# Gate copy on ScalarE, running maximum's VectorE work one step later, and six small tables in PSUM, in an attention and mixture-of-experts kernel

## The chip, the cores and the metric

One core of a Trainium2 chip runs the whole kernel. The metric is the device time of one execution in microseconds (us), and of several executions the median. The core has TensorE (PE in the profile), VectorE (DVE), ScalarE (ACT), GpSimd (POOL) and SyncE (SP), which here only issues transfers. SBUF is the large on-chip memory that all of them use; PSUM is the small one of eight banks into which TensorE writes its products, and from which VectorE and ScalarE read them.

## What is computed

```python
B, H, S, D = (8, 8, 576, 64)                      # q, k, v
scores = q @ k.T / sqrt(D)
kth    = np.partition(scores, -32)[..., -32]      # keep the 32 largest scores of a row
attn   = softmax(where(scores >= kth, scores, -1e9))
x      = (attn @ v).transpose(0, 2, 1, 3).reshape(4608, 512)
logits = x @ w_gate                               # 8 experts
e      = argmax(logits, axis=1);  p = softmax(logits)[e]
out    = p * (relu(x @ w1[e]) @ w2[e])            # F = 1024, one expert per token
```

All of it is in float32.

## The kernel before

**Attention.** The 64 heads of 8 batches give 288 units of 128 rows by 576 scores. The main loop has 144 steps (0 to 143, with a few more to drain), and each step handles two units, so that a batch is 18 steps. In step t the code issues, in this order: the exponentials of step t-4 (ScalarE, `exps`, tile `et` from the PSUM tile `tt`), the marks of step t-2 (`softmax`: ScalarE's Sign into `sg`, then GpSimd's `sb<-sb,sg` in L456), the scores of step t+3 (`scores`: TensorE into `ps`, copied by ScalarE to `sb` in L369, and the rest in L388), the product with V of step t-5 (`av`, into `px`), and the nine transposes of step t-3 (`transp`, TensorE into `tt`). Then VectorE finds the 32 largest values of each row of step t: 21 MAX8 over pieces of a row (L1026), then MAX8 and MATCH_REPLACE over the candidates (L1034).

**Small jobs.** Everything else is written as generators ("jobs") that a planner starts at due times and advances once a step. They do not issue at once: `vec(f, ...)`, `act(f, ...)`, `pe(f, ...)` and `pool(f, ...)` append to the queues `dq`, `aq`, `pq` and `gq`, and the loop empties them at fixed places. `dq` is emptied between VectorE's instructions of L1034, one job instruction behind each from the third on. All job instructions have the line of the helper, L265. The jobs that matter here:

- `j_find`, once for each batch: `r_key` from the table `idx1`; then counts on TensorE, ScalarE's `stat`, and `settle`; a step or more later `r_sl` and `r_qx` from the table `slots`.
- `settle`: `mm` (a reduce of a TensorE product in PSUM, the running maximum over the partitions), the release of the bank, and `shift` from the table `level`. A first `settle` stands in step 1 of the loop.
- `j_route`, once for each batch, behind its attention: `oh` from the table `edesc`, `hist` from the table `valid`, and `po` from the table `ebase`. It sorts the tokens to the experts.
- `j_rows`: `xm`, `lp`, `xl` and `lpl`, scaled copies out of PSUM of attention's result turned by TensorE against `turner`. The last columns of `turner` hold the gate's weights `wg`; two VectorE copies in L993, ahead of the loop, put them there.

**PSUM before.** `three` (tile `tt`, 9 blocks of 128 columns, that is 1152 float32 of a partition, 512 to a bank), `ps` (two banks), `px` (one), and two banks `pt` that jobs take and release.

**What sets the order.** Each engine runs its instructions in the order in which the code issued them, and waits on semaphores. There are no priorities. Behind the loop the flag `att_open[0]` is set to False, the last jobs run among the instructions of the experts' part, and that part runs from about 756 us to the end. It is TensorE's products of L1154 (`ph`) and L1169 (`y`), with each weight and each activation split into two parts.

Of the kernel before, what the change touches and what calls it, by code (L numbers as in the profile page):

```python
# [8 lines left out]
F32 = mybir.dt.float32  # L9
# [4 lines left out]
AF = mybir.ActivationFunctionType  # L14
OP = mybir.AluOpType
# [7 lines left out]
TOPK = 32  # L23
# [25 lines left out]
def attention_moe(ctx, tc, q, k, v, w_gate, w1, w2, out):  # L49
    nc = tc.nc  # L50
    B, H, S, D = q.shape
    HP = H // 2
    DM = H * D
    E = w_gate.shape[1]
# [11 lines left out]
    ahead, part_of = {}, []  # L66
# [5 lines left out]
    KB = MAIN + 1  # L72
# [23 lines left out]
    psum = att.enter_context(tc.tile_pool(name="psum", bufs=1, space=PSUM))  # L96
# [22 lines left out]
    turner = consts.tile([128, HP, RW], F32, name="turner")  # L119
# [8 lines left out]
    wg = consts.tile([128, DC, E], F32, name="wg")  # L128
# [128 lines left out]
    VQ, CNT, NB = {}, {}, {}  # L257
# [6 lines left out]
    def later(queue):  # L264
        return lambda f, *a, **k: queue.append(lambda: f(*a, **k))  # L265
# [13 lines left out]
    def flush(queue):  # L279
        while queue:  # L280
            queue.pop(0)()
# [16 lines left out]
        return free.pop(0)  # L298

    NB9 = 2 * MAIN + 1  # L300
    three = psum.tile([128, NB9 * 128], F32, name="tt")

    MAINS = psum.tile([128, 2, 512], F32, name="ps")

# [132 lines left out]
    def spread(pt):  # L437
        pe(nc.tensor.matmul, pt[:, 0:128], top.to_broadcast([128, 128]), ident, start=True, stop=True)

    def settle(pt, ns, done):  # L440
        mm = jobs.tile([128, 1], F32, name="mm")
        vec(nc.vector.tensor_reduce, mm, pt[:, 0:128], axis=AX.X, op=OP.max)
        vec(done)
        k = len(ns)
        vec(nc.vector.scalar_tensor_tensor, shift[:, ns[0]:ns[0] + k], slope[:, None, :].to_broadcast([128, k, 3]), mm,
            level[:, None, :].to_broadcast([128, k, 3]), op0=OP.mult, op1=OP.add)

    SHIFTED = {0, 1, 2, 3}

# [165 lines left out]
    def j_find(b):  # L615
# [2 lines left out]
        while (b + 1) * NLT // (2 * NT) - 1 not in CHECKED:  # L618
            yield
        key = sm("r_key", [128, NLT])  # L620
        vec(nc.vector.scalar_tensor_tensor, key, CNT[b], float(2 * TOPK - S), idx1, op0=OP.not_equal, op1=OP.mult)
        vec(nc.vector.max, rhs[:, :, 0], key)
        ok = sm("r_ok", [128, 9], BF)
        vec(nc.vector.tensor_scalar, ok[:, 0:8], rhs[:, :, 0], 0.0, None, op0=OP.is_gt, op1=OP.add,
# [8 lines left out]
        act(nc.scalar.activation, stat[:, b], pr[:, 0:3], AF.Copy)  # L633
        if 2 * b + 4 < NQ:
            spread(pr[:, 128:256])
            settle(pr[:, 128:256], [2 * b + 4, 2 * b + 5], leave)
            SHIFTED.update([2 * b + 4, 2 * b + 5])
        else:
            act(leave)
        yield need(slack=1)  # L640
        yield need(dve=1.3)
        sl = sm("r_sl", [128, 8], BF)
        vec(nc.vector.scalar_tensor_tensor, sl, slots[:, 0:8], stat[:, b, 0:1], ok[:, 0:8], op0=OP.add, op1=OP.mult)
        oh = sm("r_qx", [128, 512]).bitcast(BF).rearrange("p (j x) -> p j x", j=8)
        vec(nc.vector.tensor_tensor, oh, slots[:, None, :].to_broadcast([128, 8, 128]),
            sl[:, :, None].to_broadcast([128, 8, 128]), op=OP.is_equal)
        yield need(spot=1, pe=0.5)
        pl, leave = spot("li")
# [141 lines left out]
    def j_route(b):  # L790
# [19 lines left out]
        vec(nc.vector.tensor_reduce, lg, ll.rearrange("p i (h e) -> p i e h", h=H), axis=AX.X, op=OP.add)  # L810
        vec(nc.vector.tensor_reduce, mx, lg, axis=AX.X, op=OP.max)
        vec(nc.vector.tensor_tensor, sh, lg, mx[:, :, None].to_broadcast([128, KB, E]), op=OP.subtract)
        vec(nc.vector.scalar_tensor_tensor, oh, sh, 0.0, edesc, op0=OP.is_equal, op1=OP.mult)
        vec(nc.vector.tensor_reduce, fm, oh, axis=AX.X, op=OP.max)
        vec(nc.vector.tensor_tensor, oh, oh, fm[:, :, None].to_broadcast([128, KB, E]), op=OP.is_equal)
        yield need(dve=0.6)
        vec(nc.vector.tensor_tensor, hist[:, :, KB + 1:].rearrange("p e c -> p c e"), oh, valid, op=OP.mult)
        win = bass.AP(hist.tensor, hist.offset, [list(hist.ap[0]), list(hist.ap[1]), [1, KB + 1], [1, KB + 1]])
        vec(nc.vector.tensor_reduce, cum, win, axis=AX.X, op=OP.add)
        vec(nc.vector.tensor_copy, hist[:, :, KB], cum[:, :, KB])  # L820
# [12 lines left out]
        pool(nc.gpsimd.iota, pay[:, :, 3:4], pattern=[[0, KB], [0, 1]], base=0, channel_multiplier=0)  # L833
        pos = small("pos", [128, KB], I32)
        posf = small("posf", [128, KB])
        vec(nc.vector.tensor_tensor, po, po, ebase, op=OP.add)
        vec(nc.vector.tensor_tensor, po, po, oh, op=OP.mult)
        vec(nc.vector.tensor_reduce, posf, po, axis=AX.X, op=OP.add)
        vec(nc.vector.tensor_scalar, pos, posf, float(E * N - 1), None, op0=OP.min)
# [88 lines left out]
    def prep(p):  # L928
        if p < P:
            start(f"prep{p % 2}", j_prep(p))  # L930
# [47 lines left out]
        parts_w(k, [SPARE.pop(0) for _ in range(4)], nc.vector)  # L978

    SPARE = []  # L980
    prep(0)
    drain()
    prep(1)
# [5 lines left out]
            for queue in (gq, pq, aq, dq):  # L989
                flush(queue)  # L990
    drain()
    for h in range(2):
        nc.vector.tensor_copy(turner[h * D:(h + 1) * D, :, 128 + h * E:128 + (h + 1) * E], wg[h * D:(h + 1) * D])  # L993
    nc.sync.dma_start(xs[0:PAD, :], zero[:, 0:DM])
    nc.sync.dma_start(atab.rearrange("(p t) a -> p t a", p=128), attr)
    for i in range(B):
# [8 lines left out]
    for t in range(steps + LAG + TD + 4):  # L1005
        n, s = divmod(t, NT)
        if delayed:
            delayed[0](*delayed[1])
        if grp(t - LAG - TD - 1):
            exps(t - LAG - TD - 1)  # L1010
        if grp(t - LAG):
            softmax(t - LAG, grp(t - LAG), 0)
        scores(grp(t + LA))
        if grp(t - LAG):
            softmax(t - LAG, grp(t - LAG), 1)
        if grp(t - LAG - TD - 2):
            av(t - LAG - TD - 2, grp(t - LAG - TD - 2))
        scores_left(grp(t + LA))
        if grp(t - LAG - TD):
            transp(t - LAG - TD)  # L1020
        flush(pq)
        flush(aq)
        one, two, last = topk(t, grp(t)) if grp(t) else ([], [], None)
        for m in range(max(len(one), 1)):
            if m < len(one):
                one[m][0](*one[m][1])  # L1026
        delayed = last
        if t == 1:
            settle(first_pt, [0, 1, 2, 3], lambda: release(first_pt))
            mine_, dq[:] = dq[:], []  # L1030
            flush(mine_)
        mine, dq[:] = dq[:], []
        for m, (f, a) in enumerate(two):
            f(*a)  # L1034
            if mine and m >= 2:
                mine.pop(0)()
        flush(mine)
        if t == 0:
# [456 lines left out]
```

## Time and profile before

| what | value |
|---|---|
| median of 3 runs | 1278.19 us (1275.56 to 1279.88) |
| the profiled execution | 1278.04 us, of it 1276.2 us from the first to the last instruction |
| TensorE's granted clock in it, mean | 0.988 |
| busy: PE, DVE, ACT, POOL | 1209.7, 1020.9, 832.6, 840.1 us |
| VectorE's first MAX8 on scores | at 12.76 us |
| first instruction of the experts' part on TensorE (`mt`) | at 755.62 us |

In the profile a row of the timeline is: start in us, length in us, engine, line, operation, output<-inputs, sizes, count, and in brackets the idle time just ahead of it with what ended it. A group's row has the minimum, median and maximum length in ns instead. A timeline row with a count can span several instructions.

### The profile page before, as it was taken

How to read it: one execution, taken by the hardware profiler on the slowest of the kernel's cores; microseconds unless marked ns; L12 is line 12 of the kernel's file. 1: busy time of each engine (PE TensorE's matmuls, PEld its weight loads, DVE VectorE, ACT ScalarE, POOL GpSimd, SP SyncE). 2: the span in 40 equal slices, each digit the busy share in tenths (PEclk: the TensorE clock that was granted, in tenths of full speed). 3: DMA queues.
4: the chain of work that ended last, by engine and by line, in shares of the span. 5: the costliest groups of instructions: out<-in, count | busy, mean ns of one | idle time of the engine just before them, and what ended most of it. 6: DMA issues, size and time to landing. Idle time of an engine off the chain costs nothing.

```text
span 1276.2 us, 31656 instructions
## 1 busy us (share of the span) xinstructions
PE 1209.7 (95%) x9126; PEld 963.3 (75%) x9126; DVE 1020.9 (80%) x6898; ACT 832.6 (65%) x1699; POOL 840.1 (66%) x1213
## 2 busy tenths in 40 slices
PE   6999999999999999999999879899999999999997
PEld 3667667766676767666667668789899998899996
DVE  7999999999999999999999986755674333446555
ACT  4999798998898898898998853333333232333433
POOL 4676666767977967967968858766554242455654
PEclk8999999999999999999999999899999999999999
DMA  6765564654655655665654635745665243556773
GB/s 172 233 179 184 165 204 145 191 180 154 190 177 165 196 169 167 194 176 164 187 172 144 184 101 147 223 125 173 167 192 162 75 135 93 155 164 193 228 213 112
DMA packets 276758, 215.37 MB, mean 169 GB/s; under 512 B 136617, under 2 KB 218713, under 8 KB 276576
## 3 DMA queue, kind: packets, MB, share of 16 engines
q1 hardware_dynamic: 265840, 190.11, 50.5%
q0 software_dynamic: 9504, 22.86, 5.7%
q8 instruction: 74, 1.21, 0.4%
q14 instruction: 108, 0.88, 0.2%
q10 hardware_dynamic: 1232, 0.30, 0.1%
HBM read 106.69 MB, written 107.90 MB: 168 GB/s over the span
## 4 chain that ended last, share of the span: by engine, by line
DVE 43%; PE 42%; ACT 5%; POOL 4%; issue 3%; DMA 2%; SPq 1%; POOLq 0%; ACTq 0%; DVEq 0%
DVE cand L1026 21%; PE ph L1154 17%; PE y L1169 17%; DVE cand L1034 9%; DVE vq L1034 8%; PE pt L265 2%; ACT sg L455 2%; POOL sb L456 2%; PE mt L1134 1%; PE px L478 1%; PE ps L367 1%; DVE xm L265 1%; POOL wl L958 1%; PE tt L462 1%; ACT sb L369 1%
## 5 line engine op out<-in xcount | busy, mean ns | idle before, releaser
L456 POOL TENSOR_TENSOR sb<-sb,sg 128x576 f32<-128x576 f32 x288 | 370.1, 1302 | 48.3 <-ACT sg L455 41.1
L1026 DVE MAX8 cand<-sb 128x8 f32<-128x52 f32 (+2 forms) x3024 | 366.3, 207 | 0.0
L958 POOL TENSOR_TENSOR wl<-r,wh 128x512 fp32r<-128x512 f32 x118 | 153.2, 1299 | 207.2 <-DVE wh L957 201.8
L455 ACT ACTIVATE sg<-sb,nb 128x576 int8<-128x576 f32 x288 | 229.0, 795 | 49.5 <-POOL sb L456 48.9
L1155 ACT ACTIVATE hh<-ph 128x256 fp32r<-128x256 f32 (+3 forms) x136 | 58.4, 429 | 247.6 <-PE ph L1154 247.5
L478 PEld LDWEIGHTS px<-et,rv 128*64 128x64 f32 x2688 | 129.9, 137 | 119.0 <-ACT xt L265 47.6
L1034 DVE MAX8 vq<-cand 128x8 f32<-128x22 f32 (+7 forms) x1152 | 200.5, 205 | 0.0
L367 PE MATMUL ps<-qk 64*128 64x512 f32 (+1 forms) x576 | 185.0, 650 | 3.9 <-ACT sb L369 3.2
L462 PE MATMUL tt<-turner,sb 128*128 128x128 f32 x1296 | 173.5, 276 | 14.8 <-POOL sb L456 10.4
L1156 DVE SCALAR_TENSOR_TENSOR hl<-ph,hh 128x256 fp32r<-128x256 f32 (+3 forms) x136 | 65.0, 478 | 150.8 <-ACT hh L1155 150.5
L468 ACT ACTIVATE et<-tt,shift 128x1152 f32<-128x1152 f32 x144 | 178.4, 1239 | 2.9 <-PE tt L462 2.9
L478 PE MATMUL px<-et,rv 128*64 128x128 f32 (+1 forms) x2688 | 163.1, 267 | 11.4 <-ACT xt L265 8.7
L1154 PE MATMUL ph<-xh,wh 128*128 128x256 f32 (+3 forms) x536 | 169.8, 317 | 0.0
L1154 PE MATMUL ph<-xh,wl 128*128 128x256 f32 (+3 forms) x536 | 165.8, 309 | 0.0
L1154 PE MATMUL ph<-xl,wh 128*128 128x256 f32 (+3 forms) x536 | 165.3, 308 | 0.0
L462 PEld LDWEIGHTS tt<-turner,sb 128*128 128x128 f32 x1296 | 145.8, 142 | 24.9 <-POOL sb L456 18.5
L1034 DVE MATCH_REPLACE8 cand<-vq,cand 128x22 f32<-128x22 f32 (+2 forms) x864 | 158.4, 189 | 0.0
L369 ACT ACTIVATE sb<-ps 128x1024 f32<-128x1024 f32 x144 | 149.1, 1036 | 8.7 <-PE ps L367 8.5
L1169 PE MATMUL y<-wh,hl 128*128 128x512 f32 x324 | 128.3, 396 | 1.4 <-DVE hl L1156 1.4
L1169 PE MATMUL y<-wl,hh 128*128 128x512 f32 x324 | 128.2, 396 | 0.0
L1169 PE MATMUL y<-wh,hh 128*128 128x512 f32 x324 | 128.2, 396 | 0.0
L1154 PEld LDWEIGHTS ph<-xh,wh 128*128 128x128 f32 x536 | 101.7, 190 | 4.2 <-issue 1.3
(260 smaller groups left out, 2178.4 us busy)
## 6 DMA issues: line engine op xcount, KB each, us to landing
r<-in_moe_w_dram SPq DMA_DIRECT2D x236, 256.0 KB
sc<-sb SPq DMA_DIRECT2D x128, 288.0 KB
sc<-sb SPq DMA_DIRECT2D x128, 256.0 KB
rv<-in_v_dram SPq DMA_DIRECT2D x32, 256.0 KB
xs<-xm SPq DMA_DIRECT2D x16, 512.0 KB
rq<-in_q_dram SPq DMA_DIRECT2D x60, 128.0 KB
rk<-in_k_dram SPq DMA_DIRECT2D x60, 128.0 KB
sc<-sb SPq DMA_DIRECT2D x32, 144.0 KB
```

What stands on the lines that cost most here:

```text
L367: nc.tensor.matmul(MAINS[:, n], qk[:, 0, w], qk[:, 1, 2 * LEFT:], start=True, stop=True)
L369: nc.scalar.activation(bass.AP(EX[-1].tensor, EX[-1].offset, [list(EX[-1].ap[0]), [S + LEFT, 2], [1, M]]), MAINS, AF.Copy)
L455: nc.scalar.activation(upper(SG[i]), SB[u], AF.Sign, bias=nb[:, i, 1:2], accum_out=CNT[b][:, 2 * lt + i:2 * lt + i + 1])
L456: nc.gpsimd.tensor_tensor(SB[u], SB[u], SG[i], op=OP.add)
L462: nc.tensor.matmul(tt[:, c], x[:, c * 128:(c + 1) * 128], ident, start=True, stop=True, is_transpose=True)
L468: nc.scalar.activation(ET[t], three.rearrange("p (c q) -> p c q", c=NB9), AF.Exp, bias=shift[:, t // NT, 0:1], scale=0.125)
L478: yield lambda kb=kb, blk=blk: nc.tensor.matmul(px[h * 64:(h + 1) * 64], block(rv, p % 2, kb if kb < MAIN else MAIN + n, h), et[:, blk, q] ...
L958: ((other or nc.gpsimd) if i else nc.vector).tensor_tensor(lo, r, hi, op=OP.subtract)
L1026: one[m][0](*one[m][1])
L1034: f(*a)
L1154: nc.tensor.matmul(ph, a[:, c, :], x[:, c, s], start=(m == 0), stop=(m == len(seq) - 1))
L1169: nc.tensor.matmul(PY[u, t], a[:, s], x, start=(f == 0 and m == 0), stop=(f == FC - 1 and m == 2))
```

## The change

1. **Gate copy.** The two VectorE copies `turner<-wg` ahead of the loop are gone. Behind step 3 two ScalarE copies do the same.
2. **Running maximum.** In `j_find`, the instructions that `settle` gives to VectorE go to a second queue, `late_dq`, which is added to `dq` a step later. The first `settle` stands in step 2 instead of step 1.
3. **Tables.** The PSUM tile `tt` grows from 1152 to 1536 columns, three whole banks. Its last 384 columns take float32 copies of six tables (`idx1`, `slots`, `level`, `edesc`, `valid`, `ebase`; 287 columns). `const(name)` gives the PSUM copy while `att_open[0]` holds, and the SBUF table after that. ScalarE makes the copies: `level` ahead of the loop, the others with the queue that is filled in step 4. So the third bank holds the ninth transposed block of `tt` and the tables.

```diff
-    three = psum.tile([128, NB9 * 128], F32, name="tt")
+    spare = psum.tile([128, 3 * 512], F32, name="tt")
+    three = spare[:, 0:NB9 * 128]
+    TABLE = {}
+    o = NB9 * 128
+    for name, x in (("idx1", idx1), ("slots", slots), ("level", level), ("edesc", edesc), ("valid", valid), ("ebase", ebase)):
...
+        y = spare[:, o:o + n]
+        TABLE[name] = (x, y if len(x.shape) == 2 else y.rearrange("p (a b) -> p a b", b=x.shape[2]))
+        o += n
+    def const(name):
+        return TABLE[name][1 if att_open[0] else 0]
...
+    late_dq = []
-    def settle(pt, ns, done):
+    def settle(pt, ns, done, vec=vec):
...
-            level[:, None, :].to_broadcast([128, k, 3]), op0=OP.mult, op1=OP.add)
+            const('level')[:, None, :].to_broadcast([128, k, 3]), op0=OP.mult, op1=OP.add)
...
-            settle(pr[:, 128:256], [2 * b + 4, 2 * b + 5], leave)
+            settle(pr[:, 128:256], [2 * b + 4, 2 * b + 5], leave, later(late_dq))
...
-        vec(nc.vector.tensor_tensor, hist[:, :, KB + 1:].rearrange("p e c -> p c e"), oh, valid, op=OP.mult)
+        vec(nc.vector.tensor_tensor, hist[:, :, KB + 1:].rearrange("p e c -> p c e"), oh, const("valid"), op=OP.mult)
...
-        vec(nc.vector.tensor_tensor, po, po, ebase, op=OP.add)
+        vec(nc.vector.tensor_tensor, po, po, ebase if ahead and b > min(ahead) else const('ebase'), op=OP.add)
...
+    nc.scalar.activation(const("level"), level, AF.Copy)
     prep(0)
...
-    for h in range(2):
-        nc.vector.tensor_copy(turner[h * D:(h + 1) * D, :, 128 + h * E:128 + (h + 1) * E], wg[h * D:(h + 1) * D])
...
-        if t == 1:
+        if t == 2:
             settle(first_pt, [0, 1, 2, 3], lambda: release(first_pt))
             mine_, dq[:] = dq[:], []
             flush(mine_)
         mine, dq[:] = dq[:], []
+        dq += late_dq
+        late_dq.clear()
...
+        if t == 3:
+            for h in range(2):
+                r = slice(h * D, (h + 1) * D)
+                nc.scalar.activation(turner[r, :, 128 + h * E:128 + (h + 1) * E], wg[r], AF.Copy)
+        if t == 4:
+            for name in ("idx1", "slots", "edesc", "valid", "ebase"):
+                act(nc.scalar.activation, const(name), TABLE[name][0], AF.Copy)
```

`idx1` in `r_key`, `slots` in `r_sl` and `r_qx`, and `edesc` in `oh` become `const(...)` in the same way.

The order of TensorE's, GpSimd's and SyncE's instructions is the same as before. On ScalarE and VectorE three places show what moved. In these rows a name with a number is one of several buffers; `tt` as an input of a VectorE instruction is a table's copy, and what stands in brackets are the engines on whose semaphores an instruction waits.

ScalarE at the end of step 5 and the start of step 6, before:

```order
L455 ACTIVATE sg_145,cnt<-sb,nb_230 128x576 [waits Pool_49]
L388 ACTIVATE sb<-px 128x128 [waits PE_49]
L265 ACTIVATE qk_224<-pt_246 128x512 [waits PE_49]
L468 ACTIVATE et<-tt,shift 128x1152
L455 ACTIVATE sg_143,cnt<-sb,nb_230 128x576 [waits Pool_49]
```

The same place now:

```order
L471 ACTIVATE sg_145,cnt<-sb,nb_230 128x576 [waits Pool_49]
L402 ACTIVATE sb<-px 128x128 [waits PE_49]
L265 ACTIVATE tt<-idx_127 128x36 [waits PE_49,Activation_49]
L265 ACTIVATE tt<-slots 128x128 [waits Activation_49]
L265 ACTIVATE tt<-edesc 128x40 [waits Activation_49]
L265 ACTIVATE tt<-valid 128x40 [waits Activation_49]
L265 ACTIVATE tt<-ebase 128x40 [waits Activation_49]
L265 ACTIVATE qk_224<-pt_247 128x512 [waits PE_49]
L484 ACTIVATE et<-tt,shift 128x1152 [waits Activation_49]
L471 ACTIVATE sg_143,cnt<-sb,nb_230 128x576 [waits Pool_49]
```

Five table copies stand in one row there, each waiting for the one ahead of it.

VectorE in step 21, the first `mm` and `shift` of `j_find`, before:

```order
L1034 MATCH_REPLACE cand_2014<-vq,cand_2014 128x22 [waits DVE_49]
L265 TENSOR_REDUCE mm<-pt_246 128x1 [waits Activation_49]
L1034 MATCH_REPLACE cand_2015<-vq,cand_2015 128x20 [waits DVE_49]
L1034 MAX vq<-cand_2014 128x8 [waits DVE_49]
L265 SCALAR_TENSOR_TENSOR shift<-slope,mm,level 128x6 [waits DVE_49]
L1034 MAX vq<-cand_2015 128x8 [waits DVE_49]
```

Now, in step 22:

```order
L1051 MATCH_REPLACE cand_2099<-vq,cand_2099 128x22 [waits DVE_49]
L265 TENSOR_REDUCE mm<-pt_247 128x1 [waits Activation_49]
L1051 MATCH_REPLACE cand_2100<-vq,cand_2100 128x20 [waits DVE_49]
L1051 MAX vq<-cand_2099 128x8 [waits DVE_49]
L265 SCALAR_TENSOR_TENSOR shift<-slope,mm,tt 128x6 [waits DVE_49,PE_49,Activation_49]
L1051 MAX vq<-cand_2100 128x8 [waits DVE_49]
```

`mm` and `shift` stand one step later, and `shift` now waits for TensorE and ScalarE too, which write and read the same banks of `tt`. `r_key`, `r_sl`, `oh`, `hist` and one `po` have the same two new waits: for the last nine transposes and the last `et` that were issued ahead of them.

VectorE in step 20, `r_key` now (before, it waits for Activation_49 and Pool_49 alone):

```order
L1051 MAX vq<-cand_1932 128x8 [waits DVE_49]
L1051 MAX vq<-cand_1933 128x8 [waits DVE_49]
L1051 MATCH_REPLACE cand_1932<-vq,cand_1932 128x22 [waits DVE_49]
L265 SCALAR_TENSOR_TENSOR r_key<-cnt,tt 128x36 [waits PE_49,Activation_49,Pool_49]
L1051 MATCH_REPLACE cand_1933<-vq,cand_1933 128x20 [waits DVE_49]
```

The wait for PE there is for the transposes of step 17, issued in step 20.

ScalarE at the end of the attention, steps 144 and 145, before:

```order
L265 ACTIVATE xt<-px 128x256 [waits PE_49]
L468 ACTIVATE et<-tt,shift 128x1152 [waits PE_49]
L455 ACTIVATE sg_143,cnt<-sb,nb_232 128x576 [waits Pool_49]
L455 ACTIVATE sg_145,cnt<-sb,nb_232 128x576 [waits Pool_49]
L265 ACTIVATE xt<-px 128x64 [waits PE_49]
L265 ACTIVATE xt<-px 128x64
L955 ACTIVATE rv_13337<-rq 128x512 [waits DMAHW6_49]
L468 ACTIVATE et<-tt,shift 128x1152 [waits PE_49]
```

The same place now:

```order
L265 ACTIVATE xt<-px 128x256 [waits PE_49]
L484 ACTIVATE et<-tt,shift 128x1152 [waits DVE_49]
L471 ACTIVATE sg_143,cnt<-sb,nb_232 128x576 [waits Pool_49]
L471 ACTIVATE sg_145,cnt<-sb,nb_232 128x576 [waits Pool_49]
L265 ACTIVATE xt<-px 128x64 [waits PE_49]
L265 ACTIVATE xt<-px 128x64
L971 ACTIVATE rv_13343<-rq 128x512 [waits DMAHW6_49]
L484 ACTIVATE et<-tt,shift 128x1152 [waits DVE_49]
```

Nothing moved, but both `et` now wait for VectorE: the first for `oh`, which stands in VectorE's row of step 143, the second for `hist`, which follows that row. There are five or six such `et` in a batch, each behind a table's reader of the step before.

More of the change, by code (lines that the diff above doesn't have):

```diff
@@ L300, in attention_moe @@
     NB9 = 2 * MAIN + 1
-    three = psum.tile([128, NB9 * 128], F32, name="tt")
+    spare = psum.tile([128, 3 * 512], F32, name="tt")
[3 more added lines that the diff above has]
+    for name, x in (("idx1", idx1), ("slots", slots), ("level", level), ("edesc", edesc), ("valid", valid), ("ebase", ebase)):
+        n = 1
+        for d in x.shape[1:]:
+            n *= d
+        y = spare[:, o:o + n]
+        TABLE[name] = (x, y if len(x.shape) == 2 else y.rearrange("p (a b) -> p a b", b=x.shape[2]))
+        o += n
+    assert o <= 3 * 512
+    def const(name):
+        return TABLE[name][1 if att_open[0] else 0]
     MAINS = psum.tile([128, 2, 512], F32, name="ps")
@@ L620, in j_find @@
         key = sm("r_key", [128, NLT])
-        vec(nc.vector.scalar_tensor_tensor, key, CNT[b], float(2 * TOPK - S), idx1, op0=OP.not_equal, op1=OP.mult)
+        vec(nc.vector.scalar_tensor_tensor, key, CNT[b], float(2 * TOPK - S), const('idx1'), op0=OP.not_equal, op1=OP.mult)
         vec(nc.vector.max, rhs[:, :, 0], key)
@@ L642, in j_find @@
         sl = sm("r_sl", [128, 8], BF)
-        vec(nc.vector.scalar_tensor_tensor, sl, slots[:, 0:8], stat[:, b, 0:1], ok[:, 0:8], op0=OP.add, op1=OP.mult)
+        vec(nc.vector.scalar_tensor_tensor, sl, const('slots')[:, 0:8], stat[:, b, 0:1], ok[:, 0:8], op0=OP.add, op1=OP.mult)
         oh = sm("r_qx", [128, 512]).bitcast(BF).rearrange("p (j x) -> p j x", j=8)
-        vec(nc.vector.tensor_tensor, oh, slots[:, None, :].to_broadcast([128, 8, 128]),
+        vec(nc.vector.tensor_tensor, oh, const('slots')[:, None, :].to_broadcast([128, 8, 128]),
             sl[:, :, None].to_broadcast([128, 8, 128]), op=OP.is_equal)
@@ L812, in j_route @@
         vec(nc.vector.tensor_tensor, sh, lg, mx[:, :, None].to_broadcast([128, KB, E]), op=OP.subtract)
-        vec(nc.vector.scalar_tensor_tensor, oh, sh, 0.0, edesc, op0=OP.is_equal, op1=OP.mult)
+        vec(nc.vector.scalar_tensor_tensor, oh, sh, 0.0, const('edesc'), op0=OP.is_equal, op1=OP.mult)
         vec(nc.vector.tensor_reduce, fm, oh, axis=AX.X, op=OP.max)
```

## The prediction

> **What bounds the kernel now.** I read the page's busy times first, then a table of windows, because the kernel has two parts with different limits.
>
> ```profile
> span 1276.2 us, 31656 instructions
> PE 1209.7 (95%) x9126; PEld 963.3 (75%) x9126; DVE 1020.9 (80%) x6898; ACT 832.6 (65%) x1699; POOL 840.1 (66%) x1213
> ```
>
> TensorE looks like the bound, but that is an average. The windows (columns: length, then busy time of PE, PEld, DVE, ACT, POOL) tell it by stage:
>
> ```profile
> 40.00:110.00 70.00, 68.06 (x635) 49.45 (x632) 70.00 (x631) 66.18 (x134) 47.79 (x65) 1.00 0.63 192
> 150.00:450.00 300.00, 285.83 (x2555) 209.32 (x2555) 300.00 (x2597) 268.98 (x554) 231.59 (x350) 0.99 0.59 178
> 450.00:700.00 250.00, 238.29 (x2156) 175.20 (x2155) 250.00 (x2149) 222.25 (x461) 192.90 (x286) 1.00 0.58 172
> 740.00:760.00 20.00, 15.64 (x152) 12.55 (x149) 16.06 (x54) 10.31 (x21) 12.55 (x16) 0.91 0.44 119
> 920.00:1276.00 356.00, 347.71 (x2010) 314.08 (x2009) 175.69 (x327) 119.81 (x239) 166.74 (x169) 0.99 0.52 156
> ```
>
> From 150 to 700 us VectorE has no idle time at all (300.00 of 300, 250.00 of 250): in the attention each nanosecond taken from VectorE comes off the end, whatever TensorE does. The experts' part is TensorE's (347.71 of 356). Between them, around 740 to 760, nobody is full: a chain of dependences crosses the engines there. So the change has three accounts: the start, VectorE's body, and the crossing.
>
> **Part 1: the start.** Timeline rows of before:
>
> ```profile
> 11.55 1.19 DVE L993 COPY turner<-wg 64x32 f32<-64x32 f32 x2 [6.89 <-DMA wg<-in_moe_w_gate_dram]
> 12.76 1.36 DVE L1026 MAX8 cand<-sb 128x8 f32<-128x52 f32 x11
> 10.00 0.27 ACT L388 ACTIVATE sb<-px 128x128 f32<-128x128 f32 x1
> 24.75 1.03 PE L265 MATMUL pt<-turner,rq 128*128 128x128 f32 x2 [3.79 <-DMA rq<-in_q_dram]
> 27.09 0.60 ACT L265 ACTIVATE qk<-pt 128x512 f32<-128x512 f32 x1 [5.74 <-PE pt L265]
> 108.67 0.18 DVE L265 SCALAR_TENSOR_TENSOR r_key<-cnt,idx 128x36 f32<-128x36 f32 x1
> 109.10 1.15 PE L462 MATMUL tt<-turner,sb 128*128 128x128 f32 x9
> 116.71 0.29 DVE L265 TENSOR_REDUCE mm<-pt 128x1 f32<-128x128 f32 x1 [3.14 <-ACT stat L265]
> 117.17 0.76 DVE L265 SCALAR_TENSOR_TENSOR shift<-slope,mm,level 128x6 f32<-128x6 f32 x1
> ```
>
> VectorE waits 6.89 us for the gate's weights, although its first scores are complete at 10.27. Without the copies it starts at about 10.3, 2.4 us earlier. This gain doesn't last. The other engines don't start earlier: they wait for q from memory at 24.75 and 27.09, and then run full (68.06 and 66.18 us of 70 from 40 to 110). They start d later, d being the time of the copies that ScalarE now makes. ScalarE's nearest rows:
>
> ```profile
> L265 ACT ACTIVATE po<-pt x8: 190/204/205, 292.5 to 881.3; 128x40 f32<-128x40 f32 x8
> ```
>
> Four tables of 36 or 40 columns at 0.20 and one of 128 at 0.27 (the row at 10.00) are 1.1 us, each waiting for the one ahead adds some 0.3 by estimate, and the two gate copies (32 columns) 0.3: d is 1.7 us, between 0 (absorbed in ScalarE's gaps before step 20) and 2.0.
>
> VectorE then runs into `r_key` at step 20, which by the new wait needs the transposes of step 17, the row at 109.10, done at 110.25. So `r_key` goes from 108.67 to 110.25 + d, 1.58 + d later than before, and the 2.4 us are lost in that wait. Behind it the late `settle` pays. In step 21 VectorE no longer waits 3.14 us for `mm`, nor runs `mm` and the 0.76 us `shift`, some 0.96 us together; in step 22 they cost 0.55 (0.29 + 0.23 and the gap between), and their product is long there. Net behind step 22: 1.58 + d - 3.14 - 0.96 + 0.55 = d - 1.97, that is **-0.27 us** with d = 1.7, from -1.97 to 0.
>
> **Part 2: VectorE's body.** Which table readers are slow today? Group rows (minimum, median, maximum in ns), then timeline rows:
>
> ```profile
> L265 DVE TENSOR_TENSOR hist<-oh,valid x8: 321/802/5090, 284.2 to 878.1; 128x40 bf16<-128x40 f32 x8
> L265 DVE SCALAR_TENSOR_TENSOR shift<-slope,mm,level x7: 231/352/756, 20.1 to 578.8; 128x6 f32<-128x6 f32 x6, 128x12 f32<-128x12 f32 x1
> L265 DVE SCALAR_TENSOR_TENSOR r_sl<-slots,stat,r_ok x8: 212/234/253, 126.6 to 771.2; 128x8 bf16<-128x8 bf16 x8
> L265 DVE SCALAR_TENSOR_TENSOR r_key<-cnt,idx x8: 184/185/186, 108.7 to 765.0; 128x36 f32<-128x36 f32 x8
> L265 DVE TENSOR_TENSOR r_qx<-slots,r_sl x8: 1207/1208/1224, 126.9 to 771.4; 128x1024 bf16<-128x1024 bf16 x8
> L265 DVE TENSOR_TENSOR r_wk<-sg,r_sb x8: 747/952/1302, 179.8 to 802.0; 128x576 f32<-128x576 bf16 x8
> 282.34 2.51 POOL L456 TENSOR_TENSOR sb<-sb,sg 128x576 f32<-128x576 f32 x2
> 284.25 0.81 DVE L265 TENSOR_TENSOR hist<-oh,valid 128x40 bf16<-128x40 f32 x1
> 562.95 0.80 DVE L265 TENSOR_TENSOR hist<-oh,valid 128x40 bf16<-128x40 f32 x1
> L265 DVE TENSOR_TENSOR lp<-pt,rinv x48: 174/193/200, 93.7 to 797.7; 128x48 f32<-128x48 f32 x32, 128x32 f32<-128x32 f32 x16
> ```
>
> `hist` takes 0.80 us where a clear one takes 0.32: at 284.25 it starts while GpSimd's two L456 instructions run, and it ends 0.2 us behind them (284.85). `lp`, larger and with one operand in PSUM, never goes over 0.20 in 48 cases, all among the same GpSimd work. I read that as contention for SBUF between VectorE's instructions with two SBUF operands and GpSimd, from which a PSUM operand frees. Four `hist` in the loop (the first and the last are the rows at 284.25 and 562.95) go from 0.80 to about 0.25, one more from 0.32 to 0.25: 4 x 0.55 + 0.07 = **-2.25 us**, between 0 and -2.6. Five `shift` go from 0.35 to 0.23: **-0.6**. Seven `r_sl` lose 0.03 each: **-0.2**. `r_key`, `r_qx`, `oh` and `po` are close to their minimum already: 0. `r_wk` is not touched, but its 0.747 to 1.302 depends on where GpSimd stands as it starts; the phase changes, and I take +0.2, with 1.5 to each side.
>
> The new waits of the readers cost VectorE nothing in the body: a reader waits for transposes three steps back. A step lasts (745.8 - 12.76) / 144 = 5.1 us on average, and VectorE, the slowest, lags the chain. Nor should ScalarE, held in turn, starve VectorE. A hold puts `et` of step t behind a reader of step t-1, and what ScalarE issues behind it are the scores of step t+3: VectorE has three steps, some 15 us, of work left then, and ScalarE, busy 268.98 us of 300, needs less for a step than VectorE. The hold takes idle time of ScalarE, not VectorE's.
>
> A rule of the Trainium skill speaks against the tables: the page "Perfetto Trace Analysis", section "Optimizing Scalar/DVE Operations", gives VectorE about 60 ns of access overhead for an instruction on SBUF and about 125 on PSUM. On 45 readers in PSUM that would be an estimated +2.9 us. The trace disagrees so far: the 48-column `lp` from PSUM (0.20) costs 0.008 us more (medians 0.193 and 0.185) than `r_key` on 36 columns of SBUF, though it is longer.
>
> Attention in sum: -0.27 - 2.25 - 0.6 - 0.2 + 0.2 = **-3.1 us**.
>
> **Part 3: the crossing.** Steps 143 to 147:
>
> ```profile
> 738.86 1.21 ACT L468 ACTIVATE et<-tt,shift 128x1152 f32<-128x1152 f32 x1
> 744.06 0.19 DVE L265 SCALAR_TENSOR_TENSOR oh<-sh,edesc 128x40 f32<-128x40 f32 x1
> 743.36 1.22 ACT L468 ACTIVATE et<-tt,shift 128x1152 f32<-128x1152 f32 x1
> 745.80 5.09 DVE L265 TENSOR_TENSOR hist<-oh,valid 128x40 bf16<-128x40 f32 x1
> 745.70 4.97 POOL L456 TENSOR_TENSOR sb<-sb,sg 128x576 f32<-128x576 f32 x4
> 753.00 1.22 ACT L468 ACTIVATE et<-tt,shift 128x1152 f32<-128x1152 f32 x1 [0.66 <-PE tt L462]
> 755.62 0.60 PE L1134 MATMUL mt<-turner,kt 128*128 128x128 f32 x4
> 756.94 0.69 DVE L1136 TENSOR_TENSOR xl<-mt,xh 128x512 fp32r<-128x512 f32 x1 [2.04 <-ACT xh L1135]
> ```
>
> Now `et` of step 140, which ran at 738.86, must wait for `oh`, done at 744.25. It runs to 745.5; the transposes of 141 follow (1.4 us); `sg` of 142 sits behind that `et`; `et` of 141 (743.36 before) goes to about 748.2, `sg` of 143 to 749.4 and 750.3, GpSimd's last `sb`, which ended at 750.67, to 752.7. TensorE's transposes of 143, in order behind, and the last `et` (753.00) come 1.2 us later, and `mt`, behind the last `av`, 1.1 to 1.8 later: **+1.5 us**; ends 0 (the slack around 740 to 760 takes it) and +5.4 (the whole hold of 744.25 - 738.86). The 5.09 us `hist` shrinks too, but that is worth nothing: VectorE idles 2.04 us ahead of `xl`, waiting for `xh`, which waits for `mt`.
>
> In the experts' part the SBUF tables are used again and the order is as before: 0. **Sum: -3.1 + 1.5 = -1.6 us**, on 1278.04: 1276.4. The profiled execution lies 0.15 under the median of 1278.19, so I say **1276.5**.
>
> **Rivals.** A difference under 0.3% (3.8 us) can't be told from none here.
>
> *Faster.* The copies vanish in ScalarE's gaps (d = 0: -1.97), the crossing absorbs the hold (0), and `r_wk` falls on GpSimd's gaps (-1.5): -1.97 - 2.25 - 0.8 - 1.5 = -6.5, about 1271.6. For it: ScalarE is busy only 10.31 of 20 us in the crossing. Against: it and TensorE are nearly full in 40 to 110, and the L456 work fills 231.59 of 300 on GpSimd.
>
> *Slower, by the shared bank.* A reader on VectorE and the transposes with their `et` lie in one bank, so each holds the other, some six times a batch (18 steps, 92 us, in which ScalarE idles 9.5 us by its share in 150 to 450). If the holds add up to more than that idle time, and the lead of the scores is used up, VectorE starves. It decides from (3.8 + 3.1 - 1.5) / 6 = 0.9 us a batch over six batches; with 1.0, a fifth of the hold at 738.86, it is -3.1 + 1.5 + 6.0 = +4.4, 1282.5. For it: that hold of 5.4 us is certain, and six such in a batch are more than 9.5. Against: a hold only brings ScalarE nearer to VectorE, so that the next one is shorter, and VectorE's 100%.
>
> *The tables free nothing.* `hist` and `shift` are held in PSUM as in SBUF: -0.27 + 0.2 + 1.5 = +1.4, 1279.5; no row shows `hist` with a PSUM operand. The Trainium skill, "SBUF — State Buffer", section "Who interferes with whom", speaks against this rival: an instruction of VectorE with at most one SBUF input, outside the two-port modes, doesn't contend with GpSimd; the 48 `lp` agree (at most 0.20 us).
>
> *Reads from PSUM cost more.* By rows, `lp` at 0.193 against `r_key` at 0.185 bounds it at 0.01 to 0.03 for a reader, +0.5 to +1.4 over 45: 1277 to 1278; a wait that a reader newly has to pass belongs here too. The rule above ("Perfetto Trace Analysis") would give 1279.4.
>
> **Chances.** The forecast 0.42, faster 0.24, shared bank 0.14, tables free nothing 0.12, dearer reads 0.08. Only the second is faster by over 0.3% (under 1274.4), with the forecast's lower edge 0.25; only the third slower (over 1282.0), 0.13; the rest, 0.62, is within. The range reaches almost to both outer cases: 1271.0 to 1281.5. The runs shown differ by 4.3 us.
>
> **What would show it.** Right: the first MAX8 at about 10.3; no wait ahead of the first `mm`, but one of some 4 us ahead of the first `r_key`; each `hist` of the loop at about 0.25 and `shift` at 0.23; `et` at about 744 less 3 behind `oh`; `mt` at about 754. Wrong: VectorE idle anywhere between 150 and 700 us, `hist` at 0.8 again, `r_key` at the same distance from the start as the first MAX8 has, or MATMUL time of the experts' part that isn't as before.

## The result, and the profile after

The changed kernel takes 1292.69 us (median of 4, 1291.47 to 1295.18) against 1278.39 for the kernel before on the same chip: ratio 1.0118, 95% interval 1.0106 to 1.0131. It is 1.2% slower. The forecast was 1276.5 with a range of 1271.0 to 1281.5, "within 0.3%". The profiled execution took 1295.18 us, 2.5 above the median, so its span is 17.1 us longer where the medians differ by 14.3.

The page of the changed kernel, its first lines:

```profile
span 1293.3 us, 31656 instructions
PE 1212.4 (94%) x9126; PEld 968.7 (75%) x9126; DVE 1027.3 (79%) x6896; ACT 834.5 (65%) x1707; POOL 842.8 (65%) x1213
```

Nothing is much busier: VectorE has 6.4 us more, with two instructions less. The windows (columns as before):

```profile
150.00:450.00 300.00, 281.31 (x2504) 207.21 (x2503) 298.86 (x2553) 261.97 (x538) 225.97 (x339) 0.99 0.58 172
450.00:700.00 250.00, 231.60 (x2060) 170.42 (x2059) 249.71 (x2074) 215.87 (x446) 188.47 (x282) 0.99 0.57 170
740.00:760.00 20.00, 12.31 (x146) 10.16 (x144) 20.00 (x170) 11.94 (x24) 15.16 (x24) 0.93 0.39 125
```

VectorE is as full as before (298.86 of 300, 249.71 of 250) but does less: 2553 instructions in 150 to 450 us where it did 2597. So the same instructions take longer. To see where, I set the first MAX8 of each of the 144 steps against the same one of before:

| place | before, us | after, us | difference |
|---|---|---|---|
| step 0 | 12.76 | 9.99 | -2.8 |
| step 18 | 95.46 | 97.08 | +1.6 |
| step 23 | 123.77 | 124.68 | +0.9 |
| step 58 | 301.87 | 301.48 | -0.4 |
| step 71 | 367.03 | 372.74 | +5.7 |
| step 107 | 552.85 | 563.97 | +11.1 |
| step 143 | 738.99 | 755.26 | +16.3 |
| `mt`, the experts' first product | 755.62 | 774.35 | +18.7 |
| end | 1276.2 | 1293.3 | +17.1 |

Up to step 58 little is lost or won; then each batch loses 2 to 5 us, from the one on in which the routing job (`oh`, `hist`, `po`) first runs, at steps 53 to 58.

Which instructions? Group rows of the changed kernel (minimum, median, maximum in ns; `r_v` of before: the TENSOR_SCALAR 214/330/747, the SCALAR_TENSOR_TENSOR 166/168/169):

```profile
L265 DVE TENSOR_TENSOR hist<-oh,tt x6: 314/318/335, 284.8 to 764.2; 128x40 bf16<-128x40 f32 x6
L265 DVE SCALAR_TENSOR_TENSOR shift<-slope,mm,tt x7: 201/205/227, 21.8 to 594.1; 128x6 f32<-128x6 f32 x6, 128x12 f32<-128x12 f32 x1
L265 DVE TENSOR_TENSOR r_qx<-tt,r_sl x7: 1212/1215/1216, 127.8 to 694.7; 128x1024 bf16<-128x1024 f32 x7
L265 DVE TENSOR_TENSOR r_wk<-sg,r_sb x8: 746/1116/3111, 180.7 to 820.7; 128x576 f32<-128x576 bf16 x8
L265 DVE TENSOR_SCALAR r_v<-eight,r_nb x8: 214/847/992, 182.3 to 822.4; 128x8 f32<-128x8 f32 x8
L265 DVE SCALAR_TENSOR_TENSOR r_v<-r_v x8: 168/958/1105, 183.2 to 823.7; 128x8 f32<-128x8 f32 x8
```

`hist` and `shift` do what they should: never over 0.34 and 0.23 us. But `r_wk` and `r_v`, of a job that the change doesn't touch, take up to 3.1, 1.0 and 1.1 us. The timeline of step 70 shows with whom they collide, first before:

```profile
362.12 1.29 POOL L456 TENSOR_TENSOR sb<-sb,sg 128x576 f32<-128x576 f32 x1 [0.70 <-ACT sg L455]
363.79 1.37 POOL L456 TENSOR_TENSOR sb<-sb,sg 128x576 f32<-128x576 f32 x1 [0.38 <-ACT sg L455]
363.09 0.94 DVE L265 TENSOR_TENSOR r_wk<-sg,r_sb 128x576 f32<-128x576 bf16 x1
364.86 0.33 DVE L265 TENSOR_SCALAR r_v<-eight,r_nb 128x8 f32<-128x8 f32 x1
365.75 0.17 DVE L265 SCALAR_TENSOR_TENSOR r_v<-r_v 128x8 f32<-128x8 f32 x1
```

and after, the same instructions (L456 is L472 now):

```profile
365.00 2.50 POOL L472 TENSOR_TENSOR sb<-sb,sg 128x576 f32<-128x576 f32 x2
368.64 1.29 POOL L472 TENSOR_TENSOR sb<-sb,sg 128x576 f32<-128x576 f32 x1 [0.46 <-ACT sg L471]
370.31 1.28 POOL L472 TENSOR_TENSOR sb<-sb,sg 128x576 f32<-128x576 f32 x1 [0.38 <-ACT sg L471]
365.01 3.11 DVE L265 TENSOR_TENSOR r_wk<-sg,r_sb 128x576 f32<-128x576 bf16 x1
368.96 0.99 DVE L265 TENSOR_SCALAR r_v<-eight,r_nb 128x8 f32<-128x8 f32 x1
370.51 1.10 DVE L265 SCALAR_TENSOR_TENSOR r_v<-r_v 128x8 f32<-128x8 f32 x1
```

Before, `r_wk` and the first short `r_v` begin late in a GpSimd L456, so that 0.3 us of it are left, and the second `r_v` finds GpSimd done. After, GpSimd is a pair of L456 behind: `r_wk` begins 10 ns after two of them and ends 0.6 us past them, and each slow `r_v` ends within 0.03 us of the end of a L456.

Why is GpSimd behind? It waits for ScalarE's `sg`, and ScalarE is held in step 54, before and after:

```profile
275.50 1.26 ACT L468 ACTIVATE et<-tt,shift 128x1152 f32<-128x1152 f32 x1
```

```profile
280.04 1.22 ACT L484 ACTIVATE et<-tt,shift 128x1152 f32<-128x1152 f32 x1 [3.11 <-DVE oh L265]
```

This `et` is the one that must now wait until `oh` has read its table in the same bank. The waits of that kind in the changed kernel (total, times, longest):

```profile
ACT et L484 <- DVE oh L265: 20.8, 6, 5.4
ACT et L484 <- DVE hist L265: 6.1, 6, 1.3
```

Relative to VectorE's step, GpSimd's last L456 ends at +9.4 us in step 70 where it ended at +4.9. The group rows of L456, before and after, say the same of the whole loop (behind the second bar: idle time of GpSimd just before these instructions, and what ended it):

```profile
L456 POOL TENSOR_TENSOR sb<-sb,sg 128x576 f32<-128x576 f32 x288 | 370.1, 1302 | 48.3 <-ACT sg L455 41.1
L472 POOL TENSOR_TENSOR sb<-sb,sg 128x576 f32<-128x576 f32 x288 | 367.9, 1286 | 99.1 <-ACT sg L471 96.9
```

GpSimd waited 41.1 us for `sg` before and waits 96.9 now; ScalarE's `sg` waited 48.9 us for GpSimd before and waits 6.3 now. So ScalarE went from following GpSimd to holding it up. The instructions that use the shared banks take no longer themselves: an `et` 1.236 us on average (1.239 before), a transpose 0.275 (0.276).

### The profile page after: what moved, and what is told of

Read it like the earlier page. It is cut to its first block, busy times and chain, and to the rows that moved or that the text cites. A ratio compares the mean times of both kernels' runs of the same rounds, so it can differ in the third digit from the quotient of the medians.

```text
span 1293.3 us, 31656 instructions
## 1 busy us (share of the span) xinstructions
PE 1212.4 (94%) x9126; PEld 968.7 (75%) x9126; DVE 1027.3 (79%) x6896; ACT 834.5 (65%) x1707; POOL 842.8 (65%) x1213
## 4 chain that ended last, share of the span: by engine, by line
DVE 50%; PE 41%; ACT 3%; issue 2%; POOL 2%; DMA 1%; SPq 0%; POOLq 0%; ACTq 0%; DVEq 0%
DVE cand L1041 24%; PE ph L1178 17%; PE y L1193 16%; DVE cand L1051 10%; DVE vq L1051 10%; PE pt L265 2%; PE mt L1158 1%; DVE xm L265 1%; PE tt L478 1%; PE px L494 1%; PE ps L381 1%; DVE r_v L265 1%; POOL wl L974 1%; ACT sg L471 1%; DVE r_wk L265 1%
## 5 line engine op out<-in xcount | busy, mean ns | idle before, releaser
L472 POOL TENSOR_TENSOR sb<-sb,sg 128x576 f32<-128x576 f32 x288 | 367.9, 1286 | 99.1 <-ACT sg L471 96.9
L974 DVE TENSOR_TENSOR wl<-r,wh 128x512 fp32r<-128x512 f32 x118 | 101.5, 860 | 4.9 <-ACT wh L971 0.7
```

Of the source, the lines that this page charges most:

```text
L472: nc.gpsimd.tensor_tensor(SB[u], SB[u], SG[i], op=OP.add)
L974: ((other or nc.gpsimd) if i else nc.vector).tensor_tensor(lo, r, hi, op=OP.subtract)
```

## The experiments

The theory, **held ScalarE**: the readers hold ScalarE through the shared bank; ScalarE and GpSimd then run later against VectorE, and VectorE pays, either in collisions with L456 or in a wait for something that ScalarE makes. Rivals: the **start's shift** alone moves the phase; or the **freed port**, since readers in PSUM no longer stop GpSimd, which then runs at other times.

**Parts 1 and 2 without the tables.** `const` gives SBUF, no table copies:

```diff
-        return TABLE[name][1 if att_open[0] else 0]
+        return TABLE[name][0]
```

> Parts 1 and 2 alone: gate copy on ScalarE, settle's VectorE work a step later, all six tables read from SBUF, no table copies. Theory (held ScalarE: the table readers hold ScalarE's exponentials through the shared bank, ScalarE and GpSimd then run 3 to 5 us later against VectorE, and VectorE's r_wk and r_v meet GpSimd's L456): with no shared bank r_wk and r_v are as before, hist stays at 0.80 us, the start gives d - 1.97 with d of 0.4 to 1.8 us, so 1276.5 to 1278.5 us. Rival (the start's shift sets the phase): r_wk and r_v are slow here too, 1288 us or more. Rival (freed port: readers in PSUM no longer block GpSimd, so that it runs at other times): nothing is freed here, 1276.5 to 1278.5.

Measured: 1272.64 us, ratio 0.9965 (0.9953 to 0.9978), faster, and 4 us under what I expected. Step 23 comes 4.15 us earlier than before, and that is still 4.45 at step 143: without part 3 nothing is lost behind the start, and the instructions that were slow are not.

```profile
L265 DVE SCALAR_TENSOR_TENSOR r_v<-r_v x8: 166/168/168, 178.5 to 800.5; 128x8 f32<-128x8 f32 x8
```

The start of this run is another than that of the changed kernel (0.91 us later than before at step 23), so it doesn't put out the start's shift by itself. Two runs below do: part 1 alone starts step 23 0.67 us later than before and loses only 0.7 more by step 143, and the hold alone keeps the old start (0.27 us later at step 23) and is slow.

**Part 3 alone**, with the two VectorE gate copies and `settle` in step 1 put back.

> Part 3 alone: the six tables in PSUM; gate copy on VectorE ahead of the loop and settle in step 1 as before. Held ScalarE: r_wk and r_v as slow as in the changed kernel, 1289 to 1295 us. Start's shift: r_wk and r_v as before and hist at 0.1 to 0.25 us, 1275 to 1278. Freed port: as held ScalarE, 1289 to 1295.

Measured: 1291.68 us, 1.0111 (1.0094 to 1.0128). The tables alone cost what the whole change does. But VectorE pays in another coin: `r_wk` is hardly slower, and instead `mm`, which stands a step earlier here, waits for ScalarE's `stat` in five batches. The waits of VectorE in this kernel (total, times, longest):

```profile
DVE mm L265 <- ACT stat L265: 10.2, 5, 2.3
```

In the changed kernel, with part 2, there is no wait for `mm`, and the lateness shows as collisions (`r_wk` and `r_v`) instead.

**The hold alone**, on the kernel before, all tables in SBUF:

```diff
+        dq.append(lambda: HOLD.append(oh[:, 0, 0:1]) if att_open[0] else None)
...
+        dq.append(lambda: HOLD.append(hist[:, 0, KB + 1:KB + 2]) if att_open[0] else None)
...
+        while HOLD:
+            nc.scalar.activation(hold_to, HOLD.pop(0), AF.Copy)
         if grp(t - LAG - TD - 1):
             exps(t - LAG - TD - 1)
```

> The kernel before, all tables in SBUF, with one thing added: ahead of the exponentials of the step after oh, and after hist, ScalarE copies one column of oh (of hist) to a scratch tile, 0.2 us each, twelve in all in the loop; so ScalarE is held until VectorE has done that reader, without any bank shared. Held ScalarE: the holds of 3 to 5 us come back, r_wk takes over 1.2 us in some batches and r_v's instructions about 1 us, mt comes 10 to 18 us later: 1288 to 1294 us. Start's shift and freed port: only the copies are paid, on an engine with room: 1278 to 1280.

Measured: 1298.61 us, 1.0163 (1.0146 to 1.0180), 4.6 us over the upper end of what I expected. Waits of ScalarE and of VectorE (the second row is the copies of `hist`; the profile names the VectorE instruction that ran beside it):

```profile
ACT hold_to L1014 <- DVE oh L267: 28.8, 6, 6.1
ACT hold_to L1014 <- DVE cand L1040: 6.2, 5, 1.2
DVE mm L267 <- ACT stat L267: 12.7, 5, 3.6
```

Twelve copies of 0.2 us with holds at the same places (28.8 us for `oh`, 24.7 in part 3 alone), no shared bank and no table in PSUM cost more than the change, which has gains to set against them. But I expected slow `r_wk` and `r_v`, and these are as before (0.3 us in all between step 23 and 143). VectorE pays there in 9.1 us more of waiting for `mm`, and in collisions of others: `hist` 2.9 us over five, `shift` 1.6, `r_key` 1.5, `po` 1.0, `pos` 0.9. So the hold is a sufficient cause, and neither a freed port nor another start is needed for the loss; which VectorE instructions pay depends on where they stand.

**The route job's tables back in SBUF** (`edesc`, `valid`, `ebase`; `idx1`, `slots`, `level` stay in PSUM).

> The changed kernel with edesc, valid and ebase read from SBUF (oh, hist, po as before) and idx1, slots, level in PSUM: no hold by the route job, r_qx and shift still in PSUM. Held ScalarE: the large holds are gone, those of r_key, shift and r_qx stay (under 2.5 us each); r_wk and r_v near their times before: 1277 to 1281 us. Freed port: r_qx of 1.2 us a batch is the largest instruction that was freed and stays freed, so r_wk and r_v stay slow: 1286 or more. Start's shift: 1288 or more.

Measured: 1277.55 us, 1.0002 (0.9992 to 1.0012). Of the 20 us between the changed kernel and parts 1 and 2 alone, 15 are gone, though `r_qx`, the longest reader, is still in PSUM: the freed port is out here too. Holds remain (`r_key` 10.7 us in six, `shift` 3.9 in five, `r_qx` 1.1, none over 2.0), but short ones cost little: behind step 23 this kernel loses 2.2 us by step 143 against parts 1 and 2 alone, where the changed kernel loses 15.7. 4.9 us of time remain, 3.4 of them by step 23 (0.73 us earlier than before there, against 4.15).

**Only `valid` in PSUM**, so that `hist` alone holds.

```diff
-        return TABLE[name][1 if att_open[0] else 0]
+        return TABLE[name][1 if att_open[0] and name == "valid" else 0]
```

> Parts 1 and 2 with one table in PSUM, valid, so that hist alone reads PSUM and alone holds ScalarE's exponentials, once in each of six batches. Held ScalarE: in the trace of before those exponentials start up to 5 us ahead of hist's end, so the hold is 4 to 5 us each time whichever reader makes it; hist takes 0.1 us, but r_wk, r_v, po or the wait for mm pay; 1281 to 1290 us. Rival (it needs the sum of several readers' holds, one a batch is caught up): the gain of hist alone counts, 1270 to 1271.

Measured: 1281.20 us, 1.0041 (1.0025 to 1.0056), 8.6 us over the same kernel without it (0.76% by the two ratios, 9.7 us).

```profile
ACT et L484 <- DVE hist L265: 24.4, 6, 5.0
L265 DVE SCALAR_TENSOR_TENSOR r_v<-r_v x8: 167/634/1107, 179.1 to 808.1; 128x8 f32<-128x8 f32 x8
```

The hold moves to `hist` with its full length, six times 4 us. One table with one reader a batch, of 40 columns, loses several times the 2 us that it saves (`hist` 0.80 to 0.32).

**Is it GpSimd's L456 that makes the hold costly?** The changed kernel and its control (parts 1 and 2) with L456 cut to 64 columns:

```diff
-        nc.gpsimd.tensor_tensor(SB[u], SB[u], SG[i], op=OP.add)
+        nc.gpsimd.tensor_tensor(SB[u][:, 0:64], SB[u][:, 0:64], SG[i][:, 0:64], op=OP.add)
```

> Parts 1 and 2, tables in SBUF, and GpSimd's L456 cut to the first 64 of its 576 columns (the rest of the addition is left out), so that VectorE hardly meets it. It is the control for the next run. hist at 0.32 us and r_wk at 0.75 us: about 2 + 2.5 us less than with the whole L456 (1272.6), 1267 to 1270 us.

> The changed kernel with the same cut of L456. The holds on ScalarE stay, GpSimd is nearly empty in the loop. Theory (the holds cost by moving L456 onto VectorE's r_wk, r_v, po and pos): these are clean here, and what is left against the control is the start (5 us between the two at step 23) and the crossing (2.5): 5 to 9 us over the control, 1273 to 1279. Rival (the late engines themselves make VectorE wait): 15 to 20 us over the control, as without the cut.

Most scores aren't marked in these two, so the experts' part is another one (1736.02 and 1746.99 us as a whole), and my expected totals were no use. I compare up to `mt`:

| | control | changed | difference at step 143 | of it behind step 23 | difference at `mt` |
|---|---|---|---|---|---|
| L456 whole | 734.54 | 755.26 | +20.7 | +15.7 | +23.0 |
| L456 cut | 727.80 | 735.63 | +7.8 | +3.8 | +11.9 |

```profile
L265 DVE SCALAR_TENSOR_TENSOR r_v<-r_v x8: 166/168/1142, 181.5 to 802.3; 128x8 f32<-128x8 f32 x8
```

(`r_v` of the changed kernel with the cut; the median is clean, 0.17.) 12 of the 16 us behind step 23 need the whole L456. That they are collisions is read from the lengths: against its control, `r_wk`, `r_v`, `pos` and `po` together take 13.4 us longer there with the whole L456 and 0.2 us less with the cut one. The rest is mostly waits. At `mt` it lies between my 5 to 9 and the rival's 15 to 20.

**A way to keep the tables?** Third bank as a PSUM tile of its own; the exponentials of block 8 a second instruction behind the step's `sg`:

```diff
+        nc.scalar.activation(ET[t][:, 0:NB9 - 1], eight_..., AF.Exp, ...)   # at the old place
...
+        nc.scalar.activation(ET[t][:, NB9 - 1], spare[:, 0:128], AF.Exp, ...)  # behind softmax(t - LAG, ..., 1)
```

> The changed kernel with tt cut into two PSUM tiles: two banks for blocks 0 to 7, and the third bank with block 8 and the tables. The exponentials of blocks 0 to 7 wait for no table reader; those of block 8 are a second ScalarE instruction behind the step's two Sign and its copy of scores, and these wait. 144 more instructions of 0.2 to 0.3 us on ScalarE. Held ScalarE: 2.9 us of work (two sg, one sb<-ps) go ahead of the wait, so a hold of 3.5 to 5.4 us costs 0.6 to 2.5, and L456 stays nearer to its place: 1277 to 1286 us. Rival (the reads from PSUM and their waits on VectorE are what costs): no gain, 1291 or more.

Measured: 1342.95 us, 1.0510 (1.0486 to 1.0534): a miss. ScalarE's two instructions in it, and waits of VectorE:

```profile
L484 ACT ACTIVATE et<-tt,shift 128x1024 f32<-128x1024 f32 x144 | 161.1, 1119 | 4.9 <-PE tt L478 3.8
L488 ACT ACTIVATE et<-t,shift 128x128 f32<-128x128 f32 x144 | 53.2, 369 | 1.6 <-DVE oh L265 1.6
DVE xm L265 <- ACT et L484: 20.5, 6, 8.7
DVE r_key L265 <- PE pt L265: 14.1, 7, 4.0
DVE shift L265 <- PE t L478: 9.8, 6, 1.9
DVE oh L265 <- PE t L478: 6.4, 5, 1.3
```

ScalarE's wait is down to 1.6 us as meant, but 128 columns take 0.37 us, so `et` costs 214 us instead of 178, and now VectorE waits: its readers `shift` and `oh` for the late transposes of block 8 (tile `t`), `r_key` for another product of TensorE, and `xm` for ScalarE, as the profile has it. I had priced the extra instruction at 0.2 to 0.3 and forgotten whom the later transposes hold. How the 65 us over the kernel before divide among these isn't shown. The time is where the rival put it (1291 or more), but with 36 us more work on ScalarE this run says nothing for or against it.

**The two other parts by themselves.** Part 1 alone:

> Part 1 alone: gate copy on ScalarE behind step 3, settle in step 1 and in j_find as before, tables in SBUF. Theory (the start's gain is lost to the wait for mm, which ends when TensorE and ScalarE are ready, 0.4 us later by the two copies): VectorE's first MAX8 comes 2.4 us earlier, but step 22 starts 0.4 us later than before; 1278 to 1279 us, no gain. Rival (the gain of the start holds by itself): 2.4 us less, 1275.5.

Measured: 1277.09 us, 1.0004 (0.9995 to 1.0013), no gain, as expected. VectorE starts 2.7 us earlier and waits longer:

```profile
117.38 0.29 DVE L265 TENSOR_REDUCE mm<-pt 128x1 f32<-128x128 f32 x1 [4.49 <-ACT stat L265]
```

Part 2 alone:

> Part 2 alone: settle's VectorE work a step later, gate copy on VectorE ahead of the loop, tables in SBUF. Theory: the wait of 3.14 us for mm goes, mm and shift cost 0.55 instead of 0.96 us in step 22, and shift leaves GpSimd's L456, about 0.15 us in each of five batches: 3.5 + 0.75 us less, 1273 to 1274.5. Rival (the next late thing takes the place): under 1 us less, 1277.

Measured: 1275.59 us, 0.9991 (0.9980 to 1.0001), between the theory and the rival, and not told from no change. The wait for `mm` is gone and step 22 is 4.1 us earlier, but the phase is such that `shift`, `r_sl` and `r_qx` meet L456, which takes 2.9 of that back by step 24:

```profile
118.45 1.32 DVE L265 SCALAR_TENSOR_TENSOR shift<-slope,mm,level 128x6 f32<-128x6 f32 x1
124.71 2.23 DVE L265 TENSOR_TENSOR r_qx<-slots,r_sl 128x1024 bf16<-128x1024 bf16 x1
```

With part 1 these two take 0.75 and 1.22 us. So the parts' gains don't add: 0 and 0.1% alone, 0.35% together.

**Moving `hist` instead of freeing it.** Parts 1 and 2, with three empty places in `dq` ahead of `hist`:

> Parts 1 and 2 with all tables in SBUF, and three empty places in VectorE's queue ahead of hist, so that hist starts five top-k instructions (about 0.9 us) later, behind the GpSimd L456 that it meets today. Contention of two SBUF operands with GpSimd: hist falls from 0.80 to 0.32 us or less in four batches, about 2 us less than parts 1 and 2 alone (1272.6): 1270 to 1271. Rival (hist meets the next L456, or the work behind it does): no gain, 1272.5 to 1273.5.

Measured: 1272.47 us, 0.9967 (0.9954 to 0.9979).

```profile
L265 DVE TENSOR_TENSOR hist<-oh,valid x8: 324/326/5069, 282.0 to 873.6; 128x40 bf16<-128x40 f32 x8
```

`hist` is clean from SBUF, 1.9 us less over five, but the total is that without the move: between step 23 and 143 both kernels gain 0.3 us on the one before, since `r_v` (1.0 us) and short waits take back what `hist` gave. In this execution VectorE also waited 1.6 us longer at step 17. The rival was right on the total.

**The gate copies on GpSimd**, otherwise as the last one:

```diff
-                nc.scalar.activation(turner[r, ...], wg[r], AF.Copy)
+                nc.gpsimd.tensor_copy(turner[r, ...], wg[r])
```

> Parts 1 and 2 with hist three places later, tables in SBUF, and the two gate copies behind step 3 on GpSimd instead of ScalarE, which is full there. Theory: ScalarE's 0.4 us and what of VectorE's wait for xm at step 17 comes from it go: 0.4 us less than with ScalarE's copies (1272.5), 1271.5 to 1272.5. Rival (the wait at step 17 is set by the arrival of q and by ScalarE's other work): no change, 1272.5.

Measured: 1271.57 us, 0.9957 (0.9945 to 0.9970). It has the lowest median here, but its ratio is not told apart from 0.9967: the intervals overlap. Its ScalarE is 0.97 us behind that of before at step 17, where with ScalarE's copies it was 0.37 behind in parts 1 and 2 alone and 1.73 in the run above. The start differs by more from one of these to the next than the 0.4 us that the copies take, and the reason I gave isn't shown.

## Why the prediction was wrong

The failed step is the sentence of part 2 on the new waits, "The hold takes idle time of ScalarE, not VectorE's", and with it the term "`r_wk` +0.2, with 1.5 to each side". I checked only that VectorE never runs out of scores. That was right: it waits for none in 150 to 700 us. But GpSimd's L456 hangs on ScalarE, and with it the moment at which VectorE's instructions on SBUF meet it. I had named contention as what made `hist` slow, and in the crossing I had followed a held `et` on to `sg` and GpSimd's last `sb`; for the five batches of the body I did neither, and didn't ask what a later ScalarE would bring into contention. The signs that I had listed for being wrong hardly show it: VectorE idled only 1.4 us between 150 and 700, and `hist` was never slow. The loss was in the length of VectorE's other instructions: `r_wk`, `r_v`, `pos` and `po` took 14.2 us more, and waits and the rest 4.0.

The terms (from each instruction's start to the next one's, summed; those of VectorE's body between step 23 and 143):

| term | predicted | measured |
|---|---|---|
| first MAX8 | 10.3 us | 9.99 |
| d, ScalarE's delay (transposes of step 17, from 109.10 to 112.07) | 1.7 | 2.97 |
| start, d - 1.97 | -0.27 | +0.91 |
| `hist` | -2.25 | -1.95 |
| `shift`, `r_sl` | -0.8 | -0.93 |
| `r_wk` | +0.2 | +4.1 |
| `r_v`, its two slow instructions | 0 | +7.0 |
| `pos` and `po<-po,oh` | 0 | +3.1 |
| wait ahead of `skip` (3.2, step 137), semaphores, the rest | 0 | +4.0 |
| crossing | +1.5 | +2.5 |
| experts' part | 0 | -1.6 |

The formula of the start held (2.97 - 1.97 = 1.0); d was mis-sized: the five tables took 1.15 and the gate copies 0.42, but 1.4 us were there already by step 2, 0.9 of it in the prologue and 0.5 at the wait for q. Parts 1 and 2, which have no copy of `level` there, were 0.6 behind in the prologue too, so how much of it is that copy and how much differs from one execution to the next isn't told. I had priced neither. `r_key` waited 2.99 us, as foretold in kind (it started at 113.36, the transposes of step 17 ended at 113.22), and `xm` at step 17 another 4.31, which I hadn't seen.

The crossing went as the chain said: `et` of step 140 waited 5.39 us for `oh`, that of 141 0.52 for `hist`, and `mt` lost 2.5 us more than step 143 had lost, where I had forecast 1.5.

```profile
760.62 1.22 ACT L484 ACTIVATE et<-tt,shift 128x1152 f32<-128x1152 f32 x1 [5.39 <-DVE oh L265]
764.61 1.22 ACT L484 ACTIVATE et<-tt,shift 128x1152 f32<-128x1152 f32 x1 [0.52 <-DVE hist L265]
774.35 0.60 PE L1158 MATMUL mt<-turner,kt 128*128 128x128 f32 x4
```

The rival "slower, by the shared bank" had the place and the hold right, at 0.14. Its point of decision, 0.9 us a batch, was passed by far (the collisions and waits are some 18 us over five batches), but through GpSimd and not through VectorE's scores. Its argument against, that the next hold is shorter, is true of `hist` (1.3 us at most behind up to 5.4 for `oh`) and doesn't help, since each batch brings the first one again.

The rival "the tables free nothing" is out: six `hist` from PSUM never took over 0.335 us. There the rule of the Trainium skill, "SBUF — State Buffer", section "Who interferes with whom", that the prediction used (at most one SBUF input outside the two-port modes, no contention with GpSimd) was right for this kernel. The same section of the Trainium skill calls the pair of ports that VectorE shares with GpSimd an exclusive lock; `r_wk` behind two L456 (3.11 us for 0.75 of work) agrees. Dearer reads from PSUM were not seen: `r_qx` 1.215 (1.208 from SBUF), `hist` 0.318 (0.326 clear from SBUF). The Trainium skill, "Perfetto Trace Analysis", section "Optimizing Scalar/DVE Operations", puts VectorE's overhead on PSUM at about 125 ns against about 60 on SBUF; a difference of 65 ns doesn't show in these rows.

What stays open: why the experts' part is 1.6 us shorter; and whether tables in a bank without any other user would bring the 2 us of `hist` and nothing else. All eight banks are in use, so that wasn't tried.

## What to carry to other kernels

In this kernel, a table put into a bank that other engines write and read made every read of it an order between engines. Price that order by what stands behind the held instruction and what that work collides with later, not by whether the next engine starves. Where VectorE has no idle time and its instructions on SBUF grow longer under GpSimd's, as here, ask of any delay of the engine that feeds GpSimd which of VectorE's instructions it moves under GpSimd's; a cheap trial is to add the delay alone to the old kernel.

## What the runs showed of the hardware

A VectorE instruction needn't be large to lose much: TENSOR_SCALAR on 128x8 took 0.99 instead of 0.33 us, SCALAR_TENSOR_TENSOR on 128x8 1.10 instead of 0.17, and a TENSOR_SCALAR that writes 128x5 integers (`pos`) 1.00 instead of 0.17, each ending with a GpSimd L456. Two L456 in a row kept `r_wk` back for both (it ended 0.6 us behind the second). With its table in PSUM, `hist` took 0.31 to 0.34 us under a running L456, and `shift` 0.20 to 0.22.
